# Attention, convolution and mixture of experts on one core: five taps of the first group's convolution by diagonal matmuls

## The chip, the cores and the metric

The kernel runs on one core of one Trainium2 chip. The metric is the device time of one execution in microseconds (us); less is better.

## What is computed

```python
# attention and convolution, 8 batches x 8 heads, S = 256, D = 64 (d_model 512)
scores = (q @ k.T) / 8;  attn = softmax(scores);  attn_out = attn @ v
x_g = attn_out * sigmoid(glu_gate)
conv_out = depthwise convolution of x_g over the sequence, 15 taps, one weight per channel and tap
x = attn_out + conv_out * sigmoid(conv_out)
# mixture of experts over the 2048 tokens, 4 groups of 4 experts, each 512 -> 1024 -> 512
g = argmax(x @ w_group);  e = argmax(x @ w_expert[g])
out = softmax weight of g * softmax weight of e * (relu(x @ w1[g, e]) @ w2[g, e])
```

The input is fixed, the routing is not known to the program: it is computed on the chip, and the experts' weights are fetched by the numbers that come out.

## The kernel before

The 8 batches are cut into four groups of two (GS), and a group into four units of 128 channels (two heads), so there are 16 units of two batches. A unit's tile of 128 x 2 x 1024 holds q, k, the gate and v.

For each unit and batch (a pair) PE forms the scores (L336), DVE takes the negative row maximum (L358), ACT the exponentials with their sums (L363), PE transposes them (L370), ACT copies them out (L375) and PE multiplies by v (L350). DVE and ACT make the reciprocal sums (L389 to L392), PE transposes these (L403), ACT copies them (L405), and DVE scales the result to xT (L409). POOL scales k on arrival (L308) and multiplies xT by the gate (L415), which ACT has made with two operations (L317, L319).

`conv` then runs the 15 taps on DVE: one multiplication (L432) and 14 multiply-adds (L434) on 128 x 512 elements, in a PSUM bank. ACT and POOL finish the SiLU (L448 to L466). A group's four units feed its routing: L515 and L523 on PE, L518 on ACT, L539 to L604 on DVE, and SP loads the expert numbers (L610). Each batch's most frequent expert is applied to all its tokens (`dense`): weights come in eight chunks of 0.5 MB through four raw buffers, ACT and POOL split each into a high and a low part (L634, L638), PE does 96 matmuls of 256 columns (L668) and 48 of 512 (L686 to L688), ACT and DVE the relu (L699, L701), ACT the scaling of the output (L712). Tokens of the first three groups that chose another expert are gathered into three tiles of 32 slots (`Left`: L798, L821, L845, L849, L856, L859, L869) and scattered over the output by POOL (L878) once the stores of those six batches are done.

The order on each engine is not written by hand. `Flow` runs the generators as processes: each asks for an engine for an estimated time (`run`), for a buffer (`get`) or for a flag, and the engine that is free earliest takes the eligible process with the smallest key. A unit's key is its place (u.k), its convolution's is 5 or 6 higher (CD), dense has 100 and the left-over 99, so dense work takes what PE has left. The fourth argument of `run` is a slack: the step counts as ready only that much later. Where the plan leaves PE idle while dense waits, `zeros` puts filler matmuls (L249). Inside one engine the order so found is fixed in the program, and each instruction waits for its inputs in that order.

```python
CD = 5, 6, 6, 6
fl = Flow(inp=NIN, sc=3, av=1, ac=2, mo=2, pr=3, pT=3, acc=2, raw=NRAW, w=NW, ...)   # NIN = 3, NRAW = 4, NW = 5
u.ii = yield get("inp")                       # a unit's tile: three buffers
yield run("PE", 1.0, None, SL["av"])          # engine, estimate, key, slack
```

Of the kernel before, what the change touches and what calls it, by code (L numbers as in the profile page):

```python
# [186 lines left out]
def attn_conv_moe(ctx, tc, aI, cw, wr, wE, cst, out):  # L187
# [47 lines left out]
    def setup():  # L235
        s_.dma_start(out=c_sb, in_=cst)
        s_.dma_start(out=cwq, in_=cw)
        s_.dma_start(out=wr_sb, in_=wr)
# [4 lines left out]
    wz = const.tile([P, WC], BF16, name="wz")

    def zeros(hp):

# [3 lines left out]
        return emit  # L250

# [24 lines left out]
    def inputs():  # L276
# [21 lines left out]
    def unit(u):  # L298
# [16 lines left out]
        yield run("ACT", 0.1 + 0.21 * nb, u.k + 0.2)
        tg = u.t[:, 0:nb, 512:768]
        a_.activation(tg, tg, AF.Tanh, scale=0.5)  # L317
        yield run("ACT", 0.1 + 0.21 * nb, u.k + 0.2)
        a_.activation(tg, tg, AF.Copy, bias=1.0)  # L319
# [5 lines left out]
    def pair(u, i):  # L325
        t = u.t
# [53 lines left out]
    def tail(u):  # L380
# [33 lines left out]
        yield run("POOL", 0.1 + 0.57 * nb, KP)  # L414
        g_.tensor_tensor(u.xg[:, 0:nb, PAD:PAD + S], u.t[:, 0:nb, 512:768], u.xT[:, 0:nb], ALU.mult)  # L415
        fl.put("inp", u.ii)
        fl.go(conv(u), u.k + CD[u.g], fl.now[2])

    def conv(u):
# [6 lines left out]
        for k0 in range(0, KT - npl, SEG):  # L426
# [400 lines left out]
    class Left:  # L827
# [3 lines left out]
        def step(self, j, raw):  # L831
# [196 lines left out]
```

## Time and profile before

| | us |
|---|---|
| median of three runs | 406.19 |
| lowest, highest | 404.89, 409.39 |
| the profiled execution, its own time | 404.8 |
| its span, first to last instruction | 403.0 |
| PE, DVE, ACT, POOL busy | 373.5, 274.9, 261.4, 271.4 |
| granted TensorE clock, mean | 0.982 |

Busy time is a share of the whole span; the kernel has parts with different limits, so the rows below give it by stretches. A matmul's end is modelled, and a row of a short matmul between waits counts part of the wait. An f32 matmul leaves two records, a transpose or an fp32r matmul one.

### The profile page before, as it was taken

How to read it: one execution, taken by the hardware profiler on the slowest of the kernel's cores; microseconds unless marked ns; L12 is line 12 of the kernel's file. 1: busy time of each engine (PE TensorE's matmuls, PEld its weight loads, DVE VectorE, ACT ScalarE, POOL GpSimd, SP SyncE). 2: the span in 40 equal slices, each digit the busy share in tenths (PEclk: the TensorE clock that was granted, in tenths of full speed). 3: DMA queues.
4: the chain of work that ended last, by engine and by line, in shares of the span. 5: the costliest groups of instructions: out<-in, count | busy, mean ns of one | idle time of the engine just before them, and what ended most of it. 6: DMA issues, size and time to landing. Idle time of an engine off the chain costs nothing.

```text
span 403.0 us, 8853 instructions
## 1 busy us (share of the span) xinstructions
PE 373.5 (93%) x3245; PEld 297.0 (74%) x3245; DVE 274.9 (68%) x569; ACT 261.4 (65%) x582; POOL 271.4 (67%) x268
## 2 busy tenths in 40 slices
PE   8999889889999999799999979999899999988993
PEld 7555445467898777697788857897798897966982
DVE  2399999999999999999999998777255020110110
ACT  2889999987588878478698726853743544442521
POOL 2332554653499999749896757796986778199830
PEclk9899999999999999999999996999999999999999
DMA  8123243232835486442645322597687988758601
GB/s 312 52 105 114 96 151 135 104 136 83 333 111 174 145 265 211 148 157 83 231 157 178 137 78 87 177 336 235 244 279 265 302 310 289 247 160 294 230 2 56
DMA packets 22126, 72.66 MB, mean 180 GB/s; under 512 B 2310, under 2 KB 2438, under 8 KB 22080
## 3 DMA queue, kind: packets, MB, share of 16 engines
q1 hardware_dynamic: 17280, 63.43, 45.5%
q10 hardware_dynamic: 4608, 8.39, 5.5%
q8 instruction: 28, 0.46, 0.4%
q0 software_dynamic: 192, 0.24, 0.2%
q14 instruction: 18, 0.15, 0.1%
HBM read 63.62 MB, written 8.59 MB: 179 GB/s over the span
## 4 chain that ended last, share of the span: by engine, by line
PE 39%; DVE 36%; ACT 10%; issue 6%; DMA 5%; POOL 1%; SPq 1%; ACTq 0%; POOLq 0%; DVEq 0%
DVE ac L434 20%; PE sc L668 9%; PE mo L686 5%; DVE nm L358 5%; PE mo L688 5%; PE mo L687 5%; PE mo L668 4%; ACT pr L363 3%; DMA out_dram<-y 2%; PE av L350 2%; DMA in<-wE 2%; PE sc L336 2%; PE sc L869 1%; DVE ac L432 1%; DVE xT L409 1%
## 5 line engine op out<-in xcount | busy, mean ns | idle before, releaser
L638 POOL TENSOR_TENSOR wl<-raw,wh 128x512 fp32r<-128x512 f32 x128 | 161.7, 1290 | 30.3 <-ACT wh L634 29.9
L434 DVE SCALAR_TENSOR_TENSOR ac<-xg,cwq,ac 128x512 f32<-128x512 f32 x208 | 150.1, 747 | 2.3
L634 ACT CAST wh<-raw 128x1024 fp32r<-128x1024 f32 x64 | 67.0, 1047 | 32.9 <-PE mo L688 19.3
L701 DVE SCALAR_TENSOR_TENSOR hl<-sc,hh 128x512 fp32r<-128x512 f32 x18 | 12.4, 690 | 68.9 <-ACT hh L699 68.9
L363 ACT ACTIVATE pr<-sc,nm 128x256 f32<-128x256 f32 x96 | 44.8, 477 | 20.8 <-DVE nm L358 20.7
L686 PE MATMUL mo<-wh,hh 128*128 128x512 f32 x128 | 54.1, 423 | 0.0
L688 PE MATMUL mo<-wh,hl 128*128 128x512 f32 x128 | 51.2, 400 | 0.0
L687 PE MATMUL mo<-wl,hh 128*128 128x512 f32 x128 | 51.0, 398 | 0.0
L350 PE MATMUL av<-pT,in 128*64 128x256 f32 x256 | 42.6, 401 | 3.9 <-ACT pT L375 3.8
L308 POOL TENSOR_SCALAR in<-in 128x512 f32<-128x512 f32 (+1 forms) x17 | 24.2, 1421 | 28.3 <-DMA in<-aI 23.0
L358 DVE TENSOR_REDUCE nm<-sc 128x2 f32<-128x512 f32 x48 | 30.8, 680 | 7.6 <-PE sc L336 7.6
L415 POOL TENSOR_TENSOR xg<-in,xT 128x512 f32<-128x512 f32 x16 | 20.6, 1286 | 22.1 <-DVE xT L409 22.1
L370 PE MATMUL sc<-c_sb,pr 128*128 128x128 f32 x192 | 29.8, 284 | 5.3 <-ACT pr L363 4.9
L452 POOL TENSOR_TENSOR acc<-xg,acc 128x512 f32<-128x512 f32 x16 | 19.0, 1188 | 21.6 <-ACT xg L450 16.3
L350 PEld LDWEIGHTS av<-pT,in 128*64 128x64 f32 x256 | 18.3, 138 | 20.3 <-ACT pT L375 10.4
L370 PEld LDWEIGHTS sc<-c_sb,pr 128*128 128x128 f32 x192 | 21.5, 142 | 14.9 <-ACT pr L363 11.3
L375 ACT COPY pT<-sc 128x512 f32<-128x512 f32 x48 | 27.8, 595 | 5.3 <-PE sc L370 3.6
L686 PEld LDWEIGHTS mo<-wh,hh 128*128 128x128 f32 x128 | 24.6, 192 | 7.9 <-issue 3.0
L688 PEld LDWEIGHTS mo<-wh,hl 128*128 128x128 f32 x128 | 24.6, 192 | 5.8
L336 PE MATMUL sc<-in 64*128 64x256 f32 x192 | 28.5, 404 | 0.0
L687 PEld LDWEIGHTS mo<-wl,hh 128*128 128x128 f32 x128 | 24.7, 193 | 4.3
L699 ACT ACTIVATE hh<-sc 128x512 fp32r<-128x512 f32 x18 | 10.8, 598 | 23.8 <-PE sc L668 23.2
(186 smaller groups left out, 738.3 us busy)
## 6 DMA issues: line engine op xcount, KB each, us to landing
raw<-wE SPq DMA_DIRECT2D x64, 512.0 KB, 4.3
in<-aI SPq DMA_DIRECT2D x15, 1024.0 KB, 4.8
in<-wE SPq DMA_DIRECT2D x12, 1024.0 KB, 7.7
x_rows<-y ACTq DMA_DIRECT2D x16, 256.0 KB, 2.0
out_dram<-y ACTq DMA_DIRECT2D x16, 256.0 KB, 3.3
in<-aI SPq DMA_DIRECT2D x2, 512.0 KB, 4.5
c_sb<-cst SPq DMA_DIRECT2D x1, 400.0 KB, 4.0
wr_sb<-wr SPq DMA_DIRECT2D x1, 64.0 KB, 3.4
```

The source lines that it names most:

```text
L336: t_.matmul(scs[hh][:, qt, :], t[sl, i, qt * P:(qt + 1) * P], t[sl, i, 256:512], start=True, stop=True)
L350: t_.matmul(u.a[64 * hh:64 * hh + 64, i, :], u.vt[:, i, kt, hh, :], pTs[hh][1][:, kt, :], start=kt == 0, stop=kt == 1)
L358: v_.reduce_max(nm[:, hh, :], sc, axis=AX.X, negate=True)
L363: a_.activation(pr[:, qt, :], sc[:, qt, :], AF.Exp, bias=nm[:, hh, qt:qt + 1], scale=1.0, accum_out=u.sm[:, i, qt, hh, 0:1])
L370: t_.transpose(tp[:, kt, qt * P:(qt + 1) * P], pr[:, qt, kt * P:(kt + 1) * P], ident)
L434: v_.scalar_tensor_tensor(acc if k == KT - npl - 1 else ac, x, w, ac, ALU.mult, ALU.add)
L634: a_.copy(wh, raw)
L638: g_.tensor_tensor(wl[:, sl], raw[:, sl], wh[:, sl].bitcast(F32), ALU.subtract)
L668: t_.matmul(hp[:, f, :], ww[:, f, c, :], x, start=k == 0, stop=k == 11)
L686: t_.matmul(ys[t], hh[:, k, sl], w3h[:, k, :], start=j == 0 and k == 0, stop=False)
L687: t_.matmul(ys[t], hh[:, k, sl], w3l[:, k, :], start=False, stop=False)
L688: t_.matmul(ys[t], hl[:, k, sl], w3h[:, k, :], start=False, stop=j == 3 and k == 1)
```

## The change

- In the first group only (PT), the first five of the 15 taps go to PE: a matmul per tap, whose stationary matrix is the identity times that tap's weights, accumulated into the same PSUM bank. DVE's multiply-adds then start at the sixth tap.
- POOL makes these diagonals (`diags`), 128 x 512 and 128 x 128 for each of the four channel blocks, in two of the five pairs of buffers for split weights, which return after the second and the fourth unit's convolution.
- The fourth unit (RU) is loaded into two of the four raw weight buffers instead of the three unit buffers; its scaling of k, its gate and its product xg are done batch by batch.
- In the left-over tiles, the transposes (L856) and the first product of the second layer (L869 with j = 4) get a slack of 3.0 (LSL).

```diff
+PT = 5, 0, 0, 0
+LSL = 3.0
+RU = 3,
@@ setup
+        fl.set(ready0)
+    def diags():
+        yield flag(ready0)
+        yield sleep(2.5)
+        for p in range(NC if max(PT) else 0):
+            if p % 2 == 0:
+                i = yield get("w")
+                ds = [wspl.tile([P, CW], F32, name=n) for n in ("wh", "wl")]
+            d3 = ds[p % 2].rearrange("p (k m) -> p k m", m=P)
+            for k in range(0, max(PT), 4):
+                n = min(4, max(PT) - k)
+                yield run("POOL", 0.1 + 0.285 * n, DPRI)
+                g_.tensor_tensor(d3[:, k:k + n], ident.unsqueeze(1).broadcast_to([P, n, P]),
+                                 cwq[:, p, k:k + n].unsqueeze(2).broadcast_to([P, n, P]), ALU.mult)
+            dg[p] = i, d3
+            fl.set(dgf[p])
@@ inputs
-            u.ii = yield get("inp")
+            if u.n in RU:
+                u.ib, u.ii = "raw", (yield get("raw", u.nb))
+                u.ch = [(i, i + 1, wraw.tile([P, CW], F32, name="raw").unsqueeze(1)) for i in range(u.nb)]
+                for i, _, t in u.ch:
+                    yield run("SP", 1.8)
+                    s_.dma_start(out=t[:, 0], in_=aI[u.b + i, u.p])
+                fl.go(unit(u), u.k, fl.now[2] + 2.0)
+                continue
+            u.ib, u.ii = "inp", (yield get("inp"))
...
@@ unit: scaling of k, the gate, one operation for each piece of u.ch
+        for a, b, t in u.ch:
+            tg = t[:, 0:b - a, 512:768]
+            yield run("ACT", 0.1 + 0.21 * (b - a), u.k + 0.2)
+            a_.activation(tg, tg, AF.Tanh, scale=0.5)
+            yield run("ACT", 0.1 + 0.21 * (b - a), u.k + 0.2)
+            a_.activation(tg, tg, AF.Copy, bias=1.0)
...
@@ conv
-        for k0 in range(0, KT - npl, SEG):
+        npe = PT[u.g]
+        if npe:
+            yield flag(dgf[u.p])
+            for k in range(npe):
+                yield run("PE", 0.43 * nb)
+                t_.matmul(ac, dg[u.p][1][:, k, :], xg[:, 0:nb, k:k + S], start=k == 0, stop=k == npe - 1)
+            if not any(PT[u.g + 1:]):
+                dgn[u.p // 2] += 1
+                if dgn[u.p // 2] == 2:
+                    fl.put("w", dg[u.p][0])
+        for k0 in range(npe, KT - npl, SEG):
@@ Left.step
-                yield run("PE", 0.25)
+                yield run("PE", 0.25, None, LSL)
...
-                yield run("PE", 0.45)
+                yield run("PE", 0.45, None, LSL if j == 4 else 0.0)
```

The orders on the engines follow from `Flow`, so they change throughout. On DVE, at the start of the convolution (tiles: nm the maxima, dn the reciprocal sums, xT the attention result, xg_167 the first unit's gated input, xg_169 the second's), before:

```order
L409 TENSOR_TENSOR xT_168<-av,rb 128x512
L358 TENSOR_REDUCE nm<-mo 128x2 x2
L432 TENSOR_SCALAR ac<-xg_167,cwq 128x512
L434 SCALAR_TENSOR_TENSOR ac<-xg_167,cwq,ac 128x512 x3
L389 TENSOR_REDUCE dn<-sm 128x8
L390 RECIPROCAL dn<-dn 128x8
L434 SCALAR_TENSOR_TENSOR ac<-xg_167,cwq,ac 128x512 x2
L358 TENSOR_REDUCE nm<-sc 128x2 x2
L434 SCALAR_TENSOR_TENSOR ac<-xg_167,cwq,ac 128x512
```

With the change:

```order
L394 TENSOR_REDUCE nm<-mo 128x2 x2
L425 TENSOR_REDUCE dn<-sm 128x8
L426 RECIPROCAL dn<-dn 128x8
L394 TENSOR_REDUCE nm<-sc 128x2 x2
L445 TENSOR_TENSOR xT_170<-av,rb 128x512
L394 TENSOR_REDUCE nm<-mo 128x2 x2
L425 TENSOR_REDUCE dn<-sm 128x8
L426 RECIPROCAL dn<-dn 128x8
L394 TENSOR_REDUCE nm<-sc 128x2 x2
L482 SCALAR_TENSOR_TENSOR ac<-xg_167,cwq,ac 128x512 x2
L445 TENSOR_TENSOR xT_172<-av,rb 128x512
```

DVE's first tap of the first unit stood right behind the second unit's maxima (xT_168 is the first unit's result); now six more maxima and the second unit's result stand ahead of it, and it is a multiply-add, as five taps have come before it from PE.

On PE, in the second to fourth unit's attention (sc and mo are score banks, pr the exponentials, pT their transposes, rb the reciprocal sums, ac the convolution's bank), before:

```order
L370 MATMUL sc<-c_sb,pr 128x128 x8
L350 MATMUL av<-pT,in 64x256 x4
L370 MATMUL mo<-c_sb,pr 128x128 x8
L336 MATMUL sc<-in 128x256 x4
L403 MATMUL sc<-c_sb,rb 128x128 x4
L350 MATMUL av<-pT,in 64x256 x4
L336 MATMUL mo<-in 128x256 x4
L370 MATMUL sc<-c_sb,pr 128x128 x8
L350 MATMUL av<-pT,in 64x256 x4
```

With the change:

```order
L406 MATMUL sc<-c_sb,pr 128x128 x8
L469 MATMUL ac<-xg_167,wh 128x512
L386 MATMUL av<-pT,in 64x256 x4
L406 MATMUL mo<-c_sb,pr 128x128 x8
L372 MATMUL sc<-in 128x256 x4
L469 MATMUL ac<-xg_167,wh 128x512
L439 MATMUL sc<-c_sb,rb 128x128 x4
L386 MATMUL av<-pT,in 64x256 x4
L406 MATMUL sc<-c_sb,pr 128x128 x4
L372 MATMUL mo<-in 128x256 x4
L406 MATMUL sc<-c_sb,pr 128x128 x4
L469 MATMUL ac<-xg_167,wh 128x512 x2
```

L469 is a tap (its line in the changed kernel, L406 is L370's, L386 is L350's, L372 L336's, L439 L403's). The taps stand singly or in twos ahead of the value products or of the transposes of the sums.

On PE, at the first left-over tile (hs is its hidden layer, hT the transpose; wh, wl, hh, hl the split weights and hidden values of a dense batch), before:

```order
L856 MATMUL av<-c_sb,hs 128x128 x2
L686 MATMUL mo<-wh,hh 128x512
L687 MATMUL mo<-wl,hh 128x512
L688 MATMUL mo<-wh,hl 128x512
L686 MATMUL mo<-wh,hh 128x512
L687 MATMUL mo<-wl,hh 128x512
L688 MATMUL mo<-wh,hl 128x512
L869 MATMUL sc<-in,hT 32x128 x32
L686 MATMUL mo<-wh,hh 128x512
```

With the change (L904 is L856, L734 to L736 are L686 to L688, L716 is L668):

```order
L904 MATMUL av<-c_sb,hs 128x128 x2
L734 MATMUL mo<-wh,hh 128x512
L735 MATMUL mo<-wl,hh 128x512
L736 MATMUL mo<-wh,hl 128x512
L734 MATMUL mo<-wh,hh 128x512
L735 MATMUL mo<-wl,hh 128x512
L736 MATMUL mo<-wh,hl 128x512
L716 MATMUL sc<-xg_2306,wh 128x256
L716 MATMUL sc<-xg_2556,wh 128x256
L716 MATMUL sc<-xg_2677,wh 128x256
L716 MATMUL sc<-xg_2856,wh 128x256
L716 MATMUL sc<-xT_2355,wh 128x256
```

L869 came six matmuls behind the transposes; now the six are followed by 24 of the dense first layer, and L869 stands behind those.

## Rows read from the trace of the kernel before

**Rows 1.** The busy time of each engine in five stretches of the first 93 us (a row: stretch, its length, then for PE, PEld, DVE, ACT and POOL busy us and instructions, the granted TensorE clock, the share of the DMA engines, GB/s).

```profile
7.00:20.00 13.00, 11.05 (x70) 6.43 (x71) 4.95 (x10) 11.78 (x34) 4.28 (x10) 0.87 0.34 138
20.00:40.00 20.00, 18.12 (x121) 10.64 (x120) 19.79 (x34) 18.36 (x57) 7.00 (x13) 1.00 0.29 107
40.00:60.00 20.00, 16.41 (x106) 9.42 (x105) 19.72 (x35) 19.45 (x57) 11.25 (x13) 1.00 0.34 119
60.00:80.00 20.00, 17.87 (x117) 10.77 (x118) 19.86 (x36) 18.84 (x55) 10.89 (x17) 1.00 0.32 117
80.00:93.00 13.00, 11.83 (x120) 8.14 (x116) 12.85 (x22) 10.99 (x31) 7.04 (x13) 1.00 0.35 126
```

**Rows 2.** The timeline at the marks that divide the run (start us, us, engine, line, operation, out<-in, count, and in brackets the idle time before it and what ended it). L518 and L523 belong to the routing of a group: its first in this list is the first group's, its last the last group's. The last two rows are the last matmul and the last scaling before a store.

```profile
7.18 1.28 ACT L317 ACT_TABLE_LOAD   x1 [7.18 <-DMA in<-aI]
...
92.33 0.60 ACT L518 COPY y<-mo 128x512 f32<-128x512 f32 x1
...
92.98 1.07 PE L523 MATMUL mo<-c_sb,y 128*128 128x20 f32 x8
...
290.25 1.07 PE L523 MATMUL av<-c_sb,y 128*128 128x20 f32 x8 [1.40 <-ACT y L518]
...
396.29 0.40 PE L688 MATMUL mo<-wh,hl 128*128 128x512 f32 x1
...
396.72 0.69 ACT L712 ACTIVATE y<-mo,rec 128x512 f32<-128x512 f32 x1 [0.69 <-PE mo L688]
```

**Rows 3.** The same busy times in the three parts that these marks make: to the first routing, from there to the last, and from there to the last matmul (columns as in Rows 1).

```profile
0.00:93.00 93.00, 81.26 (x585) 51.28 (x585) 77.54 (x136) 79.43 (x230) 41.77 (x69) 0.98 0.36 131
93.00:290.25 197.25, 189.28 (x1755) 155.16 (x1753) 175.94 (x368) 137.93 (x293) 154.88 (x139) 0.97 0.52 179
290.25:396.70 106.45, 102.99 (x909) 90.57 (x909) 21.45 (x66) 43.31 (x60) 74.76 (x61) 1.00 0.67 230
```

**Rows 4.** Groups of instructions of DVE, whole run, and of ACT, from 7 to 93 us (line, engine, operation, out<-in, shapes, count | busy us, mean ns of one | idle time before it and its releasers).

```profile
L434 DVE SCALAR_TENSOR_TENSOR ac<-xg,cwq,ac 128x512 f32<-128x512 f32 x208 | 150.1, 747 | 2.3
L701 DVE SCALAR_TENSOR_TENSOR hl<-sc,hh 128x512 fp32r<-128x512 f32 x18 | 12.4, 690 | 68.9 <-ACT hh L699 68.9
L432 DVE TENSOR_SCALAR ac<-xg,cwq 128x512 f32<-128x512 f32 x16 | 12.0, 748 | 1.0 <-POOL xg L415 1.0
...
L363 ACT ACTIVATE pr<-sc,nm 128x256 f32<-128x256 f32 x40 | 18.7, 478 | 3.4 <-DVE nm L358 3.2
L375 ACT COPY pT<-sc 128x512 f32<-128x512 f32 x19 | 11.3, 595 | 0.7 <-PE sc L370 0.7
L317 ACT ACTIVATE in<-in 128x512 f32<-128x512 f32 x10 | 6.5, 646 | 0.0
```

**Rows 5.** Two rows of PE's timeline with f32 matmuls of 128 columns, four of which run side by side (columns as in Rows 2).

```profile
305.29 1.95 PE L869 MATMUL sc<-in,hT 128*32 128x128 f32 x64
...
339.22 1.08 PE L869 MATMUL sc<-in,hT 128*32 128x128 f32 x32
```

**Rows 6.** The filler matmuls of L249 alone, in two stretches (stretch, length, PE busy and count, PEld busy and count, clock, DMA).

```profile
7.00:93.00 86.00, 3.57 (x55) 3.24 (x55) 0.98 0.32 120
93.00:290.25 197.25, 18.91 (x280) 17.50 (x280) 0.97 0.52 179
```

**Rows 7.** The longest wait of PE's weight loads between 7 and 93 us (who <- whom: us in total, times, longest).

```profile
PEld av L350 <- ACT pT L375: 9.8, 19, 1.4
```

**Rows 8.** A group of POOL's instructions (columns as in Rows 4), and three rows of the timeline (as in Rows 2), of which the last is PE's.

```profile
L415 POOL TENSOR_TENSOR xg<-in,xT 128x512 f32<-128x512 f32 x16 | 20.6, 1286 | 22.1 <-DVE xT L409 22.1
...
9.69 1.49 POOL L308 TENSOR_SCALAR in<-in 128x512 f32<-128x512 f32 x1 [1.61 <-DMA in<-aI]
...
26.09 1.50 POOL L308 TENSOR_SCALAR in<-in 128x512 f32<-128x512 f32 x1 [4.84 <-DMA in<-aI]
...
16.07 1.16 PE L336 MATMUL sc<-in 64*128 64x256 f32 x8
```

**Rows 9.** A stretch of the chain of work that ended last, in which PE does nothing but one kind of matmul (start us, us, what, count), and the group of the transposes L493 (columns as in Rows 4).

```profile
376.95 8.73 PE sc L668 x72
...
L493 PE MATMUL sc<-c_sb,xT 128*128 128x128 f32 x64 | 9.8, 279 | 0.0
```

**Rows 10.** The timeline around 343 to 366 us: POOL, SP's DMA queue, ACT and PE (columns as in Rows 2).

```profile
351.83 1.03 POOL L878 DMA_INDIRECT out_dram<-ys,ix  x1 [8.68 <-DMA out_dram<-y]
...
355.46 2.81 SPq L615 DMA_DIRECT2D raw<-wE  x2
...
360.35 1.04 ACT L634 CAST wh<-raw 128x1024 fp32r<-128x1024 f32 x1 [4.02 <-DMA raw<-wE]
361.30 0.27 ACT L849 ACTIVATE hs<-av 128x128 f32<-128x128 f32 x1
...
361.62 0.44 PE L856 MATMUL av<-c_sb,hs 128*128 128x128 f32 x2 [1.95 <-ACT hs L849]
...
366.32 1.08 PE L869 MATMUL sc<-in,hT 128*32 128x128 f32 x32 [1.50 <-DMA in<-wE]
```

**Rows 11.** The two stretches after the start in which PE was granted less than the full clock (columns as in Rows 1), and what PE did before the second.

```profile
170.00:180.00 10.00, 10.00 (x85) 9.68 (x85) 8.86 (x19) 5.71 (x15) 4.50 (x5) 0.84 0.55 203
240.00:250.00 10.00, 8.90 (x122) 7.40 (x123) 9.55 (x22) 6.07 (x14) 5.75 (x5) 0.66 0.33 113
...
241.10 1.27 PE L798 MATMUL av<-rec,y 128*32 128x2 f32 x96 [2.28 <-DVE y L793]
```

More of the change, by code (lines that the diff above doesn't have):

```diff
@@ L60 @@
 LP = 0, 0, 0, 0
+PT = 5, 0, 0, 0
+DPRI = 0
+LSL = 3.0
+RU = 3,
 IDLE = 0.35, 0.25, 0.055
@@ L250, in zeros @@
         return emit
+    ready0 = Flag()
+    dg = [None] * NC
+    dgf = [Flag() for _ in range(NC)]
+    dgn = [0, 0]
+    def diags():
[13 more added lines that the diff above has]
+            fl.set(dgf[p])
     def warm():
@@ L282, in inputs @@
         for u in us:
-            u.ii = yield get("inp")
+            if u.n in RU:
[7 more added lines that the diff above has]
+            u.ib, u.ii = "inp", (yield get("inp"))
             u.t = inp.tile([P, MB, 1024], F32, name="in")
+            u.ch = [(0, u.nb, u.t)]
             if u.n == 0:
@@ L302, in unit @@
         g_.memset(u.sm[:, :, :, :, 1], 1e-9)
-        for i in range(0, nb, 1 if u.n == 0 else nb):
-            kk = u.t[:, i:(i + 1 if u.n == 0 else nb), 256:512]
+        u.row = [t[:, i - a] for a, b, t in u.ch for i in range(a, b)]
+        ks = [(i, i + 1, u.t[:, i:i + 1]) for i in range(nb)] if u.n == 0 else u.ch
+        for a, b, t in ks:
+            kk = t[:, 0:b - a, 256:512]
             if u.n == 0:
-                fl.now[2] = max(fl.now[2], u.half[i])
-            yield run("POOL", 0.73 * (1 if u.n == 0 else nb), KP)
+                fl.now[2] = max(fl.now[2], u.half[a])
+            yield run("POOL", 0.73 * (b - a), KP)
             g_.tensor_scalar(kk, kk, 0.125, None, ALU.mult)
-            if u.n == 0:
+            for i in range(a, b):
                 fl.go(pair(u, i), u.k + 0.1 * i, fl.now[2], "POOL")
-        u.vt = u.t.rearrange("p i f -> p i f")[:, :, 768:1024].rearrange("p i (t h d) -> p i t h d", t=2, h=2)
-        for i in range(nb if u.n else 0):
-            fl.go(pair(u, i), u.k + 0.1 * i, fl.now[2], "POOL")
         fl.go(tail(u), u.k, fl.now[2])
[L315 to L319, printed above, removed]
+        for a, b, t in u.ch:
[4 more added lines that the diff above has]
+            a_.activation(tg, tg, AF.Copy, bias=1.0)
         fl.set(u.gate)
@@ L325, in pair @@
     def pair(u, i):
-        t = u.t
+        t = u.row[i]
+        v4 = t[:, 768:1024].rearrange("p (t h d) -> p t h d", t=2, h=2)
         u.bn[i] = "mo" if u.k < NPRO and (u.q + i) % 2 else "sc"
@@ L335, in pair @@
                 sl = slice(64 * hh, 64 * hh + 64)
-                t_.matmul(scs[hh][:, qt, :], t[sl, i, qt * P:(qt + 1) * P], t[sl, i, 256:512], start=True, stop=True)
+                t_.matmul(scs[hh][:, qt, :], t[sl, qt * P:(qt + 1) * P], t[sl, 256:512], start=True, stop=True)
         pTs = [None, None]
@@ L349, in pair @@
             for hh in range(2):
-                t_.matmul(u.a[64 * hh:64 * hh + 64, i, :], u.vt[:, i, kt, hh, :], pTs[hh][1][:, kt, :],
+                t_.matmul(u.a[64 * hh:64 * hh + 64, i, :], v4[:, kt, hh, :], pTs[hh][1][:, kt, :],
                           start=kt == 0, stop=kt == 1)
@@ L413, in tail @@
         yield flag(u.gate)
-        yield run("POOL", 0.1 + 0.57 * nb, KP)
-        g_.tensor_tensor(u.xg[:, 0:nb, PAD:PAD + S], u.t[:, 0:nb, 512:768], u.xT[:, 0:nb], ALU.mult)
-        fl.put("inp", u.ii)
+        for a, b, t in u.ch:
+            yield run("POOL", 0.1 + 0.57 * (b - a), KP)
+            g_.tensor_tensor(u.xg[:, a:b, PAD:PAD + S], t[:, 0:b - a, 512:768], u.xT[:, a:b], ALU.mult)
+        for i in range(nb if u.ib == "raw" else 1):
+            fl.put(u.ib, u.ii + i)
         fl.go(conv(u), u.k + CD[u.g], fl.now[2])
@@ L953, in attn_conv_moe @@
         fl.go(warm(), -1)
+        fl.go(diags(), -1)
         fl.go(inputs(), -1)
```

## The prediction

> **What bounds the kernel now.** I first read the busy time by stretches, then the marks that cut the run into parts, then who waits inside each part, and the chain of waits for the end.
>
> Up to the first routing DVE is full. Between 20 and 80 us it is busy 19.7 to 19.9 of every 20 us, and ACT close behind with 18.4 to 19.5 [rows 1]. PE shows 16.4 to 18.1, but much of that is waiting between short matmuls: its weight loads wait 9.8 us for ACT's copies of pT alone [rows 7]. The reader should see three engines in a ring (scores, maximum, exponential, transposes, values), with the convolution as filling on DVE.
>
> Three marks divide the run [rows 2]. The first group's routing reaches PE at 92.98 us, the last group's at 290.25, and the last matmul starts at 396.29; the last output row is scaled at 396.72, and the span ends at 403.0. Between the routings DVE is busy 175.9 of 197.3 us and PE 189.3, of which 18.9 are filler matmuls that do nothing [rows 3, 6]. After the last routing PE is busy 103.0 of 106.5 us [rows 3]: there the run is as long as PE's work. So what counts is when the last routing comes, and how much of PE's work is left then.
>
> **The change part by part.** The sums are made against the profiled execution: 404.8 us with a span of 403.0, a little under the median of the runs, 406.19.
>
> *Taps off DVE.* Four units lose their first five taps: 4 multiplications of 748 ns and 16 multiply-adds of 747 [rows 4], 14.9 us, all ahead of the first routing. DVE's order up to that routing is otherwise the same work. But DVE's relief is not the gain, since ACT is next. ACT is busy 79.4 us up to 93 [rows 3] and starts at 7.18 [rows 2]. In the new order it has more in front of L518: the fourth unit's gate goes as four operations of 256 columns instead of two of 512 (4 x 0.48, by an exponential of that size, less 2 x 0.65), one copy of pT (0.60) and one of the same size from dn, some 1.8 us together [rows 4]. ACT's best stretch is 19.45 of 20 us, 97% [rows 1]. At that rate L518 comes at 7.18 + 81.2 / 0.97 = 90.9 instead of 92.33: -1.4 us. At full rate it would be 88.4, a gain of 3.9; that is the lower bound.
>
> *Taps onto PE.* No row shows a 128x512 f32 matmul over the full array. L869 is the nearest: 64 records take 1.95 us and 32 take 1.08 [rows 5], so 32 more, in four strips side by side and thus 8 deep, cost 0.87, or 0.109 per record of 128 columns. An f32 matmul is two records (L869 has 96 matmuls and 192 records), so a tap of 512 columns is 2 x 4 x 0.109 = 0.87 us, and the 20 taps 17.4. They lie beside other work if PE has that room: from 7 to 93 us it is idle 10.7 us (86 less the 75.3 busy) [rows 1] and does 3.6 us of filler [rows 6]. If PE's busy rows were all solid, 17.4 would not fit in 14.3, and the routing would come 3.1 us later: the upper bound. I take ACT's -1.4, the row it is nearest to, because PE's busy rows hold waits for ACT [rows 7].
>
> [...]
>
> *Diagonals.* POOL gets four 128x512 and four 128x128 multiplications, by L415's 1.29 us [rows 8] and a quarter of it 6.4 us. POOL is busy 41.8 of the first 93 us [rows 3], so they hide in its idle time. Five of the eight stand before the second unit's scaling of k, which began at 9.69 and whose scores PE took up at 16.07 [rows 8]; a delay of some 3 us there still arrives before it. Without that cover it would cost those 3 us. The first tap waits in PE's queue behind them and holds up the transposes and value products of the next units; they are ready far earlier, so I take nothing, and put the case in a rival.
>
> *Fourth unit in the raw buffers.* Its load leaves at once rather than after the first unit's release; before, POOL waited 4.84 us for it until 26.09 [rows 8]. DVE was full through that [rows 1], so nothing was lost then; with DVE lighter the wait would have shown, and the early load removes it. It takes two of four raw buffers until about the fifth unit, long before the first weights. I take nothing; bounds 0 and, if SP's queue put it ahead of others, one load's wait of 4.8.
>
> *Between the routings.* DVE's instructions from the first L539 to the last are 364 before and 367 after: two more L701 (0.69 each [rows 4]) and one small copy. +1.6 us if DVE is what sets this part, 0 if its idle time takes them; I take 1.6. In the same part the order has 48 more L668 and four more L493 on PE, that is dense work of later sequences done earlier, and 52 fewer fillers. 48 x 8.73/72 = 5.8 us and 4 x 9.8/64 = 0.6 [rows 9] come to 6.4; the fillers give back 52 x 18.9/280 = 3.5 [rows 6]. PE must find 2.9 us more in its 8.0 us of idle time (197.3 less 189.3 [rows 3]).
>
> *After the last routing.* Those 6.4 us of PE work are gone from a part that is as long as PE's work: -6.4.
>
> *Left-over pieces.* The slack LSL places the transposes L856 and the first L869 of each left-over tile later. Near 361 us PE waited 1.95 us for hs and 1.50 us for weights, and the root is on POOL: the scatter L878 waits 8.68 us for an output store, the splits of the weights behind it come late, SP issues the next raw load only at 355.46, ACT waits 4.02 us for it, and hs stands behind that cast [rows 10]. The scatter keeps its wait in the new order, so the jam stays; what changes is how much other work lies in front. For the third tile twelve matmuls of L686 to L688 stood between L845 and L856, now 18, which covers about half of the stall at their spacing there. I take -1.0, between -3.4 (both gone) and +3.4 (both doubled).
>
> Sum: 404.8 - 1.4 + 1.6 - 6.4 - 1.0 = 397.6 us. A measurement of this kernel can tell about 1% from no change, that is under 402.1 or over 410.3 against the median.
>
> **Rivals.**
> 1. *PE becomes the bound before the first routing* (the slower side). Each tap is 0.87 us in an in-order queue, put between transposes and value products on which ACT waits. For it: PE would carry 17.4 us more where only 14.3 are free by the rows. Against: the rows count waits as work. If three quarters of the 17.4 us end up in front of ready work, the routing comes 13.0 us later in place of 1.4 earlier: 404.8 + 13.0 + 1.6 - 6.4 - 1.0 = 412.0. It is slower than before from 5.8 us of such delay on. [...]
> 2. *The moved work is not early.* The order sets 48 matmuls ahead of the last routing, but if PE does not find the 2.9 us between the routings, DVE and the routing slip by as much as the end gains. For it: POOL is busy 154.9 of 197.3 us there [rows 3], and dense work waits for its splits. Then the term of 6.4 is 0: 404.0, no change.
> [...]
> 4. *More than I take.* ACT runs without gaps (-3.9) and both left-over stalls go (-3.4): 392.7.
>
> **How the numbers follow.** My forecast has 0.52 and would lie between 393 and 402; rival 1 has 0.10, rival 2 0.14, rival 3 0.12, rival 4 0.12. Faster by over 1%: all of rival 4, nearly all of the forecast and a third of rival 3, 0.68. Slower by over 1%: rival 1, 0.10. The rest, 0.22, is within 1%. The range is 391 to 406: it holds rivals 2, 3 and 4 and leaves out most of rival 1.
>
> **What would show it.** Right: L518 of the first group near 91 us with ACT over 95% busy from 20 to 80 us and DVE clearly below its 99%; a row of L469 near 0.87 us for a tap of two records; the last group's L523 within 2 us of 290; from there to the last matmul about 100 us instead of 106; PE waits before L856 under 1 us. Wrong: ACT's busy share falls while PE's rises before the first routing (rival 1); the last routing later by as much as the remainder is shorter (rival 2); a new stretch with the clock under 1.00 (rival 3). If the first routing came 8 us early or more, ACT was not next, and my reading of the ring was wrong.

## The result and the profile after

The changed kernel took 408.1 us (median of 20 runs, 403.5 to 412.0) against 406.35 for the kernel before (20 runs); the ratio is 1.0055, 95% interval 1.0029 to 1.0081. The forecast was 397.6 in a range of 391 to 406. By the 1% named in the prediction this is no change, but the interval leaves out 1: the changed kernel is a little slower, not faster. The ratios, here and below, leave out runs that took over 1.5% longer than the fastest of the same kernel; medians and spans hold all runs.

Single traces scatter by 1 to 2 us (the two profiled ones have spans of 402.8 after and 403.0 before, at clocks of 0.987 and 0.982), mostly with the clock that TensorE was granted: over the 88 runs of the kernel before made beside the experiments the span falls by 3.0 us per 0.01 of mean clock. Below, a "span at 0.978" is a kernel's mean span brought to that clock by this slope, with 1.96 standard errors. By it the kernel before has 403.5 ± 0.2 and the changed one 406.1 ± 0.5. It compares kernels whose runs had different clocks; where the lower clock comes with the kernel (e9, e10 and e11 have 0.972, 0.967 and 0.966 in the mean, the kernel before 0.978), the ratio is what counts.

Busy times in the stretches of [rows 1], after the change, columns as there:

```profile
7.00:20.00 13.00, 10.91 (x81) 6.74 (x78) 6.03 (x11) 12.54 (x37) 10.47 (x19) 1.00 0.56 228
20.00:40.00 20.00, 19.95 (x119) 11.51 (x118) 9.69 (x18) 17.78 (x56) 6.99 (x17) 1.00 0.30 106
40.00:60.00 20.00, 20.00 (x119) 11.36 (x118) 16.84 (x29) 17.64 (x52) 7.86 (x9) 1.00 0.16 56
60.00:80.00 20.00, 20.00 (x122) 11.49 (x120) 16.40 (x28) 18.24 (x56) 11.17 (x13) 1.00 0.32 116
80.00:93.00 13.00, 12.50 (x139) 9.20 (x138) 12.90 (x23) 10.48 (x27) 5.30 (x10) 1.00 0.38 142
```

Two things are new: PE has no gap left from 20 to 80 us, and DVE, full before, is busy 9.69 of the 20 us from 20 on, then full at the end. The marks of [rows 2] (timeline, after):

```profile
96.20 0.59 ACT L566 COPY y<-mo 128x512 f32<-128x512 f32 x1
...
97.46 1.07 PE L571 MATMUL mo<-c_sb,y 128*128 128x20 f32 x8
...
294.00 1.07 PE L571 MATMUL av<-c_sb,y 128*128 128x20 f32 x8 [1.27 <-ACT y L566]
...
395.56 0.39 PE L736 MATMUL mo<-wh,hl 128*128 128x512 f32 x1
```

The first routing comes 3.87 us later (96.20 for 92.33 at ACT's copy), the last 3.75 later, the last matmul 0.73 earlier. The parts of [rows 3], after:

```profile
0.00:97.50 97.50, 93.59 (x663) 58.55 (x663) 66.64 (x117) 80.88 (x234) 47.51 (x79) 1.00 0.34 125
97.50:294.00 196.50, 187.09 (x1748) 153.65 (x1746) 176.09 (x369) 139.01 (x292) 161.28 (x145) 0.99 0.55 188
294.00:396.50 102.50, 98.67 (x856) 85.71 (x856) 20.27 (x64) 41.81 (x58) 67.93 (x55) 0.98 0.64 225
```

The granted clock fell in other places than before. The changed kernel has 0.91 and 0.92 from 210 to 230 us, between the routings, and once more behind the last (busy times, after):

```profile
350.00:360.00 10.00, 7.17 (x68) 6.02 (x67) 1.38 (x2) 3.34 (x5) 9.67 (x8) 0.91 0.90 320
360.00:370.00 10.00, 10.00 (x68) 7.89 (x67) 0.00 (x0) 3.80 (x5) 5.38 (x5) 0.92 0.87 329
```

The kernel before had 0.84 and 0.66 between the routings [rows 11] and 1.00 behind the last [rows 3].

The chain of waits from 20 us on is PE alone, 59 us without a gap, then DVE (start us, us, what, count):

```profile
20.20 1.13 PE ac L469 x2
...
24.60 1.06 PE ac L469 x2
...
78.37 0.88 PE ac L469 x2
79.25 0.03 issue
79.27 0.77 DVE ac L482
```

A tap (L469, two records) is 1.06 us of it where it stands alone. Its groups on PE (columns as in [rows 4]), 20.4 us for 20 taps:

```profile
L469 PE MATMUL ac<-xg,wh 128*128 128x512 f32 x20 | 10.3, 619 | 0.0
L469 PE MATMUL ac<-xg,wl 128*128 128x512 f32 x20 | 10.1, 608 | 0.0
```

And DVE over the stretch in which it was full before (timeline, after):

```profile
22.87 0.17 DVE L425 TENSOR_REDUCE dn<-sm 128x8 f32<-128x16 f32 x1 [2.88 <-ACT pr L399]
...
24.63 1.29 DVE L394 TENSOR_REDUCE nm<-sc 128x2 f32<-128x512 f32 x2 [1.35 <-PE sc L372]
27.23 0.69 DVE L445 TENSOR_TENSOR xT<-av,rb 128x512 f32<-128x512 f32 x1 [1.31 <-PE av L386]
28.79 1.29 DVE L394 TENSOR_REDUCE nm<-mo 128x2 f32<-128x512 f32 x2 [0.87 <-PE mo L372]
...
34.20 1.29 DVE L394 TENSOR_REDUCE nm<-sc 128x2 f32<-128x512 f32 x2 [1.88 <-PE sc L372]
35.41 1.54 DVE L482 SCALAR_TENSOR_TENSOR ac<-xg,cwq,ac 128x512 f32<-128x512 f32 x2
```

The kernel before has its first tap here (its timeline):

```profile
21.16 0.76 DVE L432 TENSOR_SCALAR ac<-xg,cwq 128x512 f32<-128x512 f32 x1
```

DVE's sum for the first unit begins 14.25 us later, and DVE was relieved of 14.9 us. It idles until then, waiting for scores and exponentials, because the sum is behind the five taps and the order spreads those over four passes of the attention.

### The profile page after: what moved, and what is told of

Same layout as the page of the kernel before. It is cut to its first block, busy times and chain, and to the rows that moved or that the text cites. A ratio compares the mean times of both kernels' runs of the same rounds, so it can differ in the third digit from the quotient of the medians.

```text
span 402.8 us, 8879 instructions
## 1 busy us (share of the span) xinstructions
PE 379.4 (94%) x3263; PEld 297.9 (74%) x3263; DVE 263.0 (65%) x549; ACT 261.9 (65%) x584; POOL 276.7 (69%) x278
## 4 chain that ended last, share of the span: by engine, by line
PE 57%; DVE 17%; ACT 9%; DMA 6%; POOL 6%; issue 3%; SPq 0%; ACTq 0%; POOLq 0%; DVEq 0%
PE sc L716 9%; DVE ac L482 8%; PE mo L734 6%; PE mo L716 6%; PE mo L735 5%; PE mo L736 5%; PE av L386 5%; PE ac L469 5%; POOL wl L686 4%; PE sc L372 3%; PE sc L406 3%; ACT pr L399 2%; DVE nm L394 2%; DMA in<-wE 2%; ACT wh L682 2%
## 5 line engine op out<-in xcount | busy, mean ns | idle before, releaser
L686 POOL TENSOR_TENSOR wl<-raw,wh 128x512 fp32r<-128x512 f32 x128 | 161.8, 1290 | 38.7 <-ACT wh L682 38.6
L482 DVE SCALAR_TENSOR_TENSOR ac<-xg,cwq,ac 128x512 f32<-128x512 f32 x192 | 139.7, 749 | 4.8 <-PE ac L469 2.2
L734 PE MATMUL mo<-wh,hh 128*128 128x512 f32 x128 | 53.5, 418 | 0.0
L736 PE MATMUL mo<-wh,hl 128*128 128x512 f32 x128 | 50.8, 397 | 0.0
L345 POOL TENSOR_SCALAR in<-in 128x512 f32<-128x512 f32 (+1 forms) x16 | 22.6, 1415 | 21.7 <-DMA in<-aI 21.5
L452 POOL TENSOR_TENSOR xg<-in,xT 128x512 f32<-128x512 f32 x15 | 19.3, 1284 | 24.3 <-DVE xT L445 24.3
L406 PE MATMUL sc<-c_sb,pr 128*128 128x128 f32 x192 | 29.9, 283 | 5.0 <-ACT pr L399 4.6
L386 PE MATMUL av<-pT,in 128*64 128x256 f32 x240 | 33.6, 400 | 0.4 <-DVE ix L858 0.4
L406 PEld LDWEIGHTS sc<-c_sb,pr 128*128 128x128 f32 x192 | 21.1, 141 | 16.0 <-ACT pr L399 10.8
L734 PEld LDWEIGHTS mo<-wh,hh 128*128 128x128 f32 x128 | 24.5, 191 | 7.4 <-issue 2.5
L736 PEld LDWEIGHTS mo<-wh,hl 128*128 128x128 f32 x128 | 24.5, 191 | 5.6
L372 PE MATMUL sc<-in 64*128 64x256 f32 x184 | 26.1, 402 | 0.0
L386 PEld LDWEIGHTS av<-pT,in 128*64 128x64 f32 x240 | 15.2, 139 | 13.2 <-issue 3.9
```

The lines of the kernel that those rows point to most:

```text
L372: t_.matmul(scs[hh][:, qt, :], t[sl, qt * P:(qt + 1) * P], t[sl, 256:512], start=True, stop=True)
L386: t_.matmul(u.a[64 * hh:64 * hh + 64, i, :], v4[:, kt, hh, :], pTs[hh][1][:, kt, :], start=kt == 0, stop=kt == 1)
L406: t_.transpose(tp[:, kt, qt * P:(qt + 1) * P], pr[:, qt, kt * P:(kt + 1) * P], ident)
L482: v_.scalar_tensor_tensor(acc if k == KT - npl - 1 else ac, x, w, ac, ALU.mult, ALU.add)
L686: g_.tensor_tensor(wl[:, sl], raw[:, sl], wh[:, sl].bitcast(F32), ALU.subtract)
L734: t_.matmul(ys[t], hh[:, k, sl], w3h[:, k, :], start=j == 0 and k == 0, stop=False)
```

## The experiments

The expectations speak of "the first routing's add"; L518 (L566) is ACT's copy of the logits, and that copy is meant. Theory 1 is PE's time for the taps; theory 2 the order; theory 3, formed after eight runs, DVE's late start behind the taps. The matmuls that they count behind the last routing are all of PE's there, not dense ones alone, and where e2's speaks of 31 taps there are 15, all on DVE. In the table the copy is also given with the start taken out: the work began up to 2.3 us later in some traces, and 1.2 us earlier in e12, so "from the start" is the copy's time less what the first exponential came later than the 9.01 us of the kernel before. (e6, whose order is that of before up to there, confirms it: 92.6 for 92.3.)

| kernel | ratio to before, 95% | mean clock | span at 0.978 | first tap on DVE | copy | from the start |
|---|---|---|---|---|---|---|
| before | 1 | 0.978 | 403.5 ± 0.2 | 21.16 | 92.33 | 92.3 |
| changed | 1.0055 [1.0029, 1.0081] | 0.978 | 406.1 ± 0.5 | 35.41 | 96.20 | 96.0 |
| e1 taps only | 1.016 [1.010, 1.021] | 0.981 | 410.4 ± 1.2 | 32.63 | 95.83 | 94.9 |
| e2 no taps | 1.011 [1.008, 1.014] | 0.978 | 405.8 ± 0.5 | 20.21 | 90.66 | 90.4 |
| e3 cheap taps | 0.997 [0.993, 1.001] | 0.979 | 402.8 ± 0.6 | 37.92 | 96.84 | 94.6 |
| e4 double taps | 1.053 [1.044, 1.062] | 0.976 | 423.6 ± 0.7 | 39.42 | 113.16 | 113.0 |
| e5 raw buffers only | 1.025 [1.019, 1.031] | 0.973 | 411.1 ± 1.0 | 20.11 | 90.58 | 90.4 |
| e6 slack only | 1.001 [0.997, 1.005] | 0.977 | 403.9 ± 0.8 | 23.70 | 94.90 | 92.6 |
| e7 taps and raw | 1.012 [1.006, 1.017] | 0.979 | 407.9 ± 1.0 | 35.69 | 96.48 | 96.0 |
| e8 free taps | 1.000 [0.996, 1.004] | 0.980 | 404.3 ± 0.9 | 36.41 | 95.32 | 93.3 |
| e9 split sums | 0.997 [0.992, 1.002] | 0.972 | 398.5 ± 0.4 | 20.26 | 88.25 | 87.9 |
| e10 split, cheap | 1.019 [1.006, 1.031] | 0.967 | 405.8 ± 1.0 | 20.04 | 95.22 | 95.2 |
| e11 split, free | 0.996 [0.990, 1.002] | 0.966 | 395.1 ± 0.6 | 22.20 | 87.77 | 87.2 |
| e12 two taps | 0.990 [0.985, 0.995] | 0.981 | 398.8 ± 0.9 | 21.70 | 86.24 | 87.5 |
| e13 ten taps | 0.982 [0.976, 0.989] | 0.980 | 401.4 ± 1.0 | 23.60 | 89.97 | 89.3 |
| e14 split, late | 1.002 [0.998, 1.005] | 0.982 | 405.7 ± 0.8 | 35.23 | 102.01 | 101.9 |

**The parts one by one (e1, e2, e5, e6, e7).** The changed kernel with these constants:

```diff
 # changed: PT = 5, 0, 0, 0   RU = 3,   LSL = 3.0
+# e1: RU = ()  LSL = 0.0          e2: PT = 0, 0, 0, 0
+# e5: PT = 0, 0, 0, 0  LSL = 0.0  e6: PT = 0, 0, 0, 0  RU = ()
+# e7: LSL = 0.0
```

> The changed kernel with its taps and diagonals, but the fourth unit back in the input buffers and no slack for the left-over pieces. Theory 1 (TensorE's throughput between 20 and 79 us, which the 20 us of taps fill up, delays the first routing): the delay stays, since the taps are all there: the add that ends the first routing's sigmoid (L518 in the kernel before, 92.3 us) comes at 95 to 99, TensorE busy 20 of 20 us in 20:60, and the whole is 0 to 2% above the kernel before. Theory 2 (the fourth unit's early start in the raw buffers puts work of a later unit ahead, and this and not the taps delays the routing): that add comes at 92 or earlier, and the whole is 1% below the kernel before.

> The changed kernel with no tap on TensorE (all 31 on VectorE and GpSimd as before), with the fourth unit in the raw buffers and the slack for the left-over pieces kept. Theory 1 (the taps fill TensorE): the first routing's add (92.3 us before, 96.2 in the changed kernel) is back at 91 to 93, TensorE's busy share of 20:80 falls to 16 to 18 of 20 us, and the whole is within 1% of the kernel before. Theory 2 (the other two parts delay the routing): it stays at 95 or later and the whole is that of the changed kernel or above it.

> The kernel before with one part of the change: the fourth unit in the raw weights' buffers (no taps on TensorE, no slack). In its order 53 dense matmuls stand behind the last routing that stood ahead of it before (922 in place of 869). Theory A (those matmuls are TensorE's work that is only put later, where the run is as long as TensorE's work): the first routing's add comes at 90 to 92, the remainder after the last routing is 4 to 6 us longer than the 106.5 before, and the whole is 0.4 to 1.2% above the kernel before. Theory B (the early load is free, the changed kernel's loss is the taps' alone): the whole is within 0.3% of the kernel before or under it.

> The kernel before with one part of the change: the slack for the left-over pieces (no taps, the fourth unit in the input buffers). The order up to the last routing is that of the kernel before. Forecast of the prediction: -1.0 us, between -3.4 and +3.4; TensorE's waits before the transposes of the left-over tiles (1.95 and 1.50 us near 361 us before) are under 1 us. Theory A (that is worth what it takes out of the remainder): 0.2 to 0.6% below the kernel before. Theory B (what TensorE does not wait there it waits elsewhere): within 0.2%.

> The changed kernel without the slack for the left-over pieces: taps and the fourth unit in the raw buffers. Theory A (the slack is worth about 1 us): 0.2 to 0.6% above the changed kernel. Theory B (the slack is worth nothing): within 0.2% of it. Against the run with the taps alone, it says what the fourth unit's early load is worth beside the taps: if it is that load that makes the taps bearable, this run is 0.8% or more under that one.

Without taps the copy is back at 90.4 (e2, e5), with them at 95 to 96 (e1, e7): the delay comes with the taps, as theory 1 of e1 and e2 has it, and the early load even gains 1.9 us there. Yet no part is faster alone; e2's whole is 1.1% above the kernel before, where I expected less than 1%. In e5 the part from the last routing to the last matmul is 112.5 us for the 106.0 of before:

```profile
289.33 1.42 PE L571 MATMUL av<-c_sb,y 128*128 128x20 f32 x8 [1.85 <-ACT y L566]
...
304.09 0.95 PE L846 MATMUL av<-rec,y 128*32 128x2 f32 x94
...
401.80 0.40 PE L736 MATMUL mo<-wh,hl 128*128 128x512 f32 x1
```

(timeline, e5). Theory A of e5 named 53 dense matmuls put behind the last routing, by [rows 9] 53 x 8.73 / 72 = 6.4 us, and the remainder is longer by just that. This is chance: the trace has the same 360 matmuls of L716 and 192 of L734 to L736 there as the kernel before has of L668 and L686 to L688. The 53 are 48 small ones of the left-over tiles (L846, two records each, some 1 us in all), four transposes (L541) and one more. PE idles some 1.7 us more there than before, and the clock is 0.84 from 290 to 300 us and 0.83 from 370 to 380, worth 3.3 us of full-speed work by an estimate, 10 us x 0.16 and 10 us x 0.17. Why the whole is 2.5% longer (expected 0.4 to 1.2) stays open.

The slack alone is worth nothing (e6, +0.4 ± 0.8; theory B held): PE no longer waits before the transposes (L904), but 2.50 us for weights at L893 near 365 us and 1.28 at L917 near 383. The changed kernel waits 2.83 at L893. With taps and raw buffers it is -1.8 (changed against e7, theory A), and e7 is 0.6% under e1 where I asked for 0.8. The parts don't add; each has an order of its own.

**Cheap, double and free taps (e3, e4, e8), in the order of the changed kernel.** In e3 the taps' operands, gated input and diagonals, are rounded to fp32r.

```diff
-t_.matmul(ac, dg[u.p][1][:, k, :], xg[:, 0:nb, k:k + S], ...)          # changed
+t_.matmul(ac, dg[u.p][1][:, k, :], u.xr[:, 0:nb, k:k + S], ...)        # e3: both operands F32R
+t_.matmul(ac, zf, xg[:, 0:nb, k:k + S], start=False, stop=...)         # e4: second matmul, zf = 0
 # e8: no matmul; VectorE's tap at k == npe is a tensor_scalar
```

> [...] Theory 1 (TensorE's time for the taps): TensorE gets back 10 to 13 us, ScalarE is next, the first routing's add comes at 87 to 91 in place of 96.2, and the whole is 397 to 401 us, 1 to 2% below the changed kernel. Theory 2 (the order that the taps bring, with the waits for VectorE's last ten taps of the fourth unit): the add stays within 1.5 us of 96.2 and the whole within 0.5% of the changed kernel.

> The changed kernel, and behind each of the 20 taps a second matmul of the same size with a matrix of zeros, added into the same sum; all else in the same order. That is 20 us more of TensorE work (20 x 1.0). Theory 1 (TensorE is full from 20 to 79 us): the first routing's add comes 14 to 20 us later than the 96.2 of the changed kernel, and the whole 12 to 20 us later. Theory 2 (TensorE's busy rows hold waits, and it is the order that costs): under 5 us later.

> The changed kernel in its own order on all engines, but the 20 tap matmuls are left out: the first group's convolution lacks its first five taps, and VectorE's first operation of each unit starts the sum. The diagonals are still made. So it is the change with taps that cost nothing. Theory 1 (TensorE's time for the taps holds up the first routing, and each microsecond of that goes to the end): with 20 us gone from a TensorE that was full for 59 us, ScalarE or VectorE sets the pace; the first routing's add comes at 88 to 92 in place of 96.2 and the whole 5 to 8 us below the changed kernel. Theory 2 (it is the order: VectorE has the ten taps of the fourth unit left at the end whatever TensorE does): the add comes at 94 or later and the whole within 2 us of the changed kernel.

Double taps: the copy 17.0 us later, the whole 17.5 at equal clock. In e4's chain of waits an added matmul (L472) is 0.86 us, 17.2 for the 20. So PE is the bound there: its added time counts in full, and what the first routing loses the end loses. But the other direction saturates at once. With 20 us of PE's work gone (e8), PE has gaps again and the copy wins 2.7 us:

```profile
20.00:40.00 20.00, 17.86 (x118) 10.29 (x114) 10.55 (x20) 19.00 (x61) 8.01 (x17) 1.00 0.28 106
```

(busy times, e8). DVE is still half empty there, its first tap still at 36.41. Theory 1's 88 to 92 was wrong; of theory 2's two figures the copy was near (93.3 for 94 or later) and the whole 1.8 us under the changed kernel at equal clock. In e3 a tap is one record of 0.46 us in the mean, 8.3 us for the 20 against 20.4 (L474, groups of PE, 7 to 97 us), so PE got 12.1 us back. e3 met neither of its theories in full: at the copy it lies between (1.4), in all it is 3.3 under the changed kernel, more than e8 (1.5 more, with ± 1.0), and no run says why.

**The late start (e9, e11, e14).** VectorE sums its ten taps by itself and adds PE's five at the end:

```diff
+            fl.go(taps(u, ac), u.k + CD[u.g], fl.now[2])   # the five taps, a routine of their own
-                if k == 0:
-                    v_.tensor_scalar(ac, x, w, None, ALU.mult)
+                if k == npe:
+                    v_.tensor_scalar(to, x, w, None, ALU.mult)   # to: acc in SBUF
...
+        if npe:
+            yield flag(u.pt)        # e14: this wait ahead of VectorE's loop instead
+            v_.tensor_tensor(acc, acc, ac, ALU.add)
 # e11: as e9 without the matmul; the last line is a tensor_scalar on acc
```

> The changed kernel, but VectorE does not wait for TensorE's five taps: it sums its own ten in SBUF from the moment the gated input is there, and adds TensorE's sum of five at the end, one more operation of about 0.7 us per unit (2.8 us in all). The order is planned anew (763 dense matmuls after the last routing in place of 816). Theory 3 (the relief of VectorE's 14.9 us is eaten because its first tap starts only at 35.4 us in place of 21.2, behind five taps that the order spreads between the attention's matmuls; TensorE's own time for the taps costs a part on top): VectorE's first tap starts at 20 to 23 us and the first routing's add, 96.2 in the changed kernel, comes 4 us or more earlier, at 88 to 92. Theory 1 (TensorE is full with the taps until 79 us whatever VectorE does): the add stays at 95 to 98.

> The run with separate sums in its own order on all engines, but the 20 tap matmuls are left out (the first group's convolution lacks its first five taps; the last addition is one of the same size on VectorE's own sum). Against that run it is TensorE's price of the taps alone; against the run with free taps in the changed kernel's order, which had the first routing's add at 95.3, it is VectorE's late start alone. Theory 3: 85 to 90. Theory 1 (with TensorE relieved the order does not matter): 94 to 96, as in that run.

> The run with separate sums (first routing's add at 88.2, span 399.0 at a clock of 0.978), with one difference in what it asks for: VectorE starts a unit's sum only when TensorE's five taps for it are done. The extra addition per unit stays. The order is planned anew (889 dense matmuls after the last routing). Theory 3 (the wait costs 7 to 8 us): VectorE's first tap at 34 to 37 us, the add back at 95 to 99, and the whole 5 us or more above the run with separate sums. If it was the new order or the bank and not the wait: the add at 88 to 91.

First tap and copy in the timelines of e9, e11 and e14:

```profile
20.26 0.61 DVE L487 TENSOR_SCALAR acc<-xg,cwq 128x512 f32<-128x512 f32 x1 [0.20 <-POOL xg L452]
...
88.25 0.58 ACT L578 COPY y<-mo 128x512 f32<-128x512 f32 x1
```

```profile
22.20 0.61 DVE L486 TENSOR_SCALAR acc<-xg,cwq 128x512 f32<-128x512 f32 x1
...
87.77 0.58 ACT L577 COPY y<-mo 128x512 f32<-128x512 f32 x1
```

```profile
35.23 0.48 DVE L488 TENSOR_SCALAR acc<-xg,cwq 128x512 f32<-128x512 f32 x1
...
102.01 0.58 ACT L578 COPY y<-mo 128x512 f32<-128x512 f32 x1
```

With all 20 taps at their price but DVE free to begin, the copy comes 8.0 us earlier than in the changed kernel. Put the wait back (e14) and that is lost: +14.0 at the copy. The taps' price is 0.8 us at the copy beside an early start (e9 against e11), perhaps more, as e11's trace has a lower clock (0.91 from 40 to 60 us, e9 1.00). e14 and e9 were each planned anew, so the 14.0 is not the wait's price alone, and e14's copy lies 6 us behind the changed kernel's; the late first tap is common to both. In all, e9's median is 5.0 us under the changed kernel's (403.1 for 408.1) and 2.5 under e14's, where I expected 5 or more; at equal clock it is 7.6 and 7.2. Against the kernel before the ratio of 0.997 is no clear gain. The difference is its clock, 0.972 for 0.978 and 0.982; its trace has 0.83 from 160 to 170 and from 230 to 240 us. Its order holds 122 filler matmuls of L254 and the changed one 313; that the clock falls for want of them was not tried. At the first routing theory 3 is what the runs bear out.

**ScalarE next? (e13)** The order of before, five taps left out:

```diff
+LOW = 5, 0, 0, 0
+                if k < LOW[u.g]:
+                    continue
-                if k == 0:
+                if k == LOW[u.g]:
```

> The kernel before in its own order on all engines, with the first five taps of the first group's convolution left out on VectorE and put nowhere: 20 operations of 748 ns less, no diagonals, no tap on TensorE, no wait. So it is the relief of VectorE alone. The prediction's step (ScalarE is next): the first routing's add, 92.3 us before, comes at 88.4 to 90.9. If the ring of scores, maximum, exponential and transposes sets the pace by its waits and not by one engine: 91 to 92.3. If VectorE's relief counts in full: under 85.

The copy at 89.3 from the start, where the prediction put 88.4 to 90.9, with ACT busy 19.84 of the 20 us from 40 on (busy times, e13):

```profile
40.00:60.00 20.00, 17.16 (x114) 10.30 (x112) 17.15 (x30) 19.84 (x57) 11.68 (x15) 1.00 0.37 136
```

So 14.9 us off DVE are worth 3.0 us at the copy and 2.1 in all at equal clock (± 1.1; the medians are 402.6 and 405.3), before anything is paid for them.

**Two versions (e10, e12).** e10 is e9 with the operands of e3 and a price of 0.24 in place of 0.43; e12 is the changed kernel with two taps, put into PE's queue at once:

```diff
-PT = 5, 0, 0, 0
+PT = 2, 0, 0, 0                                  # e12
-                yield run("PE", 0.43 * nb)
+                yield run("PE", 0.43 * nb, -5)   # e12
```

> As the run with separate sums, but with the taps' operands rounded to fp32r, so that a tap takes about 0.48 us in place of 1.06 (0.86), and planned at that price; the first group's gated input loses low bits of its mantissa. Theory 3 with both causes taken away: VectorE's first tap at 20 to 23 us, TensorE with room, ScalarE next: the first routing's add at 85 to 90, and the whole 1 to 2.5% below the kernel before. If the add is early and the whole is not, what is won before the first routing is lost behind it.

> The changed kernel with two taps per unit on TensorE in place of five, and put into its queue as soon as the gated input is there (before any attention work that waits); the order is planned anew, with 871 dense matmuls after the last routing (869 in the kernel before). VectorE loses 8 operations (6.0 us), TensorE gains 8 taps of about 1 us. Theory 3: VectorE's first tap starts at 23 to 26 us, some 3 us late for 6 us of relief, and the first routing's add comes at 89 to 92.5; the whole within 1% of the kernel before. Theory 1: at 92 to 94 (a delay in the proportion of the taps, two fifths of 4).

e10 failed its expectation. Cheap taps were planned early in PE's queue, and one stood at its head before its input was there (PE's timeline, e10):

```profile
41.71 0.80 PE L467 MATMUL ac<-xg,wh 128*128 128x512 f32 x1 [2.93 <-POOL xg L457]
42.44 1.98 PE L391 MATMUL av<-pT,raw 128*64 128x256 f32 x8
```

Behind it the value products waited, ACT did 13.91 us of work in the 20 from 40 on, and PE's granted clock was 0.83 there. That this stall is all of the 7 us between e10 and e9 at the copy was not tried. e12 is the version that beats both kernels, by about 1%: 0.990 of before [0.985, 0.995], 399.9 us against 405.4, and its copy, at 87.5, is earlier than any theory had it. Of the 4.8 us at the copy the early load alone brings 1.9 (e5); the taps bring 2.9 beside it (e2, another order). DVE's first tap waits 1.63 us for PE's two, and comes at 21.70, before the 23 to 26 I expected:

```profile
21.70 0.75 DVE L482 SCALAR_TENSOR_TENSOR ac<-xg,cwq,ac 128x512 f32<-128x512 f32 x1 [1.63 <-PE ac L469]
...
86.24 0.58 ACT L566 COPY y<-mo 128x512 f32<-128x512 f32 x1 [0.32 <-PE mo L563]
```

(timeline, e12).

## Why the prediction was wrong

**The step that failed: "DVE's order up to that routing is otherwise the same work".** The work is the same, but it starts 14.25 us later. The order shown with the change has it in plain sight (six more maxima ahead of DVE's first tap, five taps of PE before it), and I read it as a move and priced only the instructions. The prediction did name a first tap that waits in PE's queue, but as a load on the attention, and took nothing for it. The term of -1.4 was +3.6 from the start. In steps: DVE's relief -3.0 (e13); the late start, with the rest of the new order, +4.0 (from e13 to e8); PE's price +2.7 (from e8 to the changed kernel). The first and the last are measured within one order; the middle one spans two orders, and in the pairs that differ in the start it is 6.1 (e8, e11), 8.0 (changed, e9) and 14.0 (e9, e14), so its sign is shown and that it is no small term, its size is not.

**ScalarE next** was right as a limit on the relief (e13): 3.0, between the 1.4 I took and the bound of 3.9. The 1.4 holds 1.8 us of new work on ACT that e13 does not have; without it the prediction's rate gives 7.18 + 79.4 / 0.97 = 89.0, and e13 has 89.3. In the changed kernel ACT never became the limit: it is busy 17.6 to 18.2 of 20 us.

**Taps onto PE.** The tap is 1.02 us where I had 0.87. That PE's busy rows hold waits was right: 20.4 us went into a PE that had shown 52.4 of 60 us busy, and cost 2.7 us, inside the bound of 3.1, though I had taken nothing. That holds up to the point where PE has no gap left: from there e4 pays 17.0 us for the 17.2 added.

**Rival 1** had the engine and the signs right (ACT's share falls, PE's rises to 20.0 of 20 us), but not the price: its 13.0 us of delay were 2.7, and a cause that was none of my rivals came beside it.

**Diagonals:** POOL's busy time from 7 to 20 us rose by 6.2 us (forecast 6.4), in its idle time; the second unit's scores were not held up (PE took them up at 14.79 us, before at 16.07).

**Fourth unit:** I took nothing; by e5 the early load alone brings the copy 1.9 us forward. In that order the whole is 7.6 us longer at equal clock, for a reason that stays open.

**Between and after the routings, left-over:** by the marks -0.7 for the +1.6 of the forecast, and -4.5 for its -6.4 - 1.0 = -7.4. The sum, -5.2 for -5.8, is near by luck: one term was 2.3 too high, the other 2.9 too low. The 48 matmuls did move (312 of L716 stand behind the last routing, 360 of L668 before). Much of both misses is, by an estimate, the granted clock, rival 3 in the last line of the prediction: 10 us x 0.16 and 10 us x 0.34 [rows 11] are 5.0 us of full-speed work that the kernel before lost between the routings, and by its stretches above the changed one lost 1.7 there and 1.7 behind the last. Without that the terms would be +2.6 and -6.2.

Of the 7.0 us between the forecast of 397.6 and the profiled execution of the changed kernel (404.6), then, 5.9 stand at the first routing (L523 4.5 later for 1.4 earlier), -2.3 between the routings, +2.9 behind the last and +0.5 behind the last matmul. The median is 3.5 us higher; 2.8 of that, by the slope above, is the high clock of the profiled execution. Of the 2.8 us by which the profiled pair (-0.2) and the runs (+2.6 at equal clock) differ, 1.5 are the pair's clocks by the same slope; the rest is within the scatter of single traces.

## What to carry to other kernels

In these runs work taken off a full engine helped only from the moment at which the engine could start on what was left: 14.9 us were taken off DVE, its first tap came at 35.41 us for 21.16, and the copy 3.6 us later from the start. If the moved part stands first in a chain (here a running sum), look for when the other engine's queue hands it over: here that became the start of the whole chain. Give the moved part a sum of its own and add late (e9, 8.0 us at the first routing against the changed kernel), or move less and issue it at once (e12). Read a reordered queue for when the first dependent instruction can start, and price that, before counting instructions.

## What was not expected of the hardware

An f32 tap of 128x512 on 128*128 is two records of 0.59 us, 1.06 us in the chain alone and 0.86 each for two in a row (L469, the changed kernel); with fp32r operands it is one record of 0.46 (L474, e3). DVE's multiply-add took 881 ns in the mean with its sum in SBUF and 750 with it in PSUM (groups of DVE, e9, 7 to 97 us), so e9 paid 36 x 0.13 = 4.7 us and four more additions for its early start:

```profile
L489 DVE SCALAR_TENSOR_TENSOR acc<-xg,cwq,acc 128x512 f32<-128x512 f32 x36 | 31.6, 881 | 0.5
L489 DVE SCALAR_TENSOR_TENSOR ac<-xg,cwq,ac 128x512 f32<-128x512 f32 x16 | 11.6, 750 | 0.2
```

The mean hides two cases. The median in SBUF is 750 ns too, but six of the 36 took 1.40 to 1.68 us. Each of the six began while POOL ran a TENSOR_TENSOR on tiles in SBUF (L512, L515 or L526), and ended some 0.55 us after it. Here are two of them with POOL's (timeline, e9; x3 is those two and one of 0.75 us):

```profile
38.88 1.17 POOL L512 TENSOR_TENSOR acc<-xg,acc 128x512 f32<-128x512 f32 x1
39.06 4.01 DVE L489 SCALAR_TENSOR_TENSOR acc<-xg,cwq,acc 128x512 f32<-128x512 f32 x3
40.13 1.60 POOL L515 TENSOR_TENSOR xT<-xT,acc 128x512 f32<-128x512 f32 x1
```

With the sum in PSUM none took over 0.76 us, in e9 or in the changed kernel, where POOL ran a TENSOR_TENSOR beside most of them (151 of the 192 L482). So in e9 the price of the sum in SBUF stands in the six operations beside POOL's: of the 31.6 us of the 36 they took some 9.7, an estimate from the starts and lengths in the timeline, which leaves 0.73 us for each of the other 30.
